# A long convolution beside a gated MLP: tokens by half-sequences, outer transforms in small array tiles, parameters in two plain loads, a new instruction order

## The chip, the core and the metric

One core of one Trainium2 chip. The metric is the device time of one execution in microseconds; the program runs on core 0 alone. What the host does with the arrays before the launch is not in it.

## What is computed

```python
xn = layernorm(A_u)                           # 2048 tokens x 512 channels, bf16
dt = exp(log_dt)[:, None]
K  = einsum("dn,dnl,dn->dl", C, exp(dt * A * l), dt * B).real   # A, B, C complex, 512 x 128
y  = irfft(rfft(pad(xn)) * rfft(pad(K)))[:2048] + xn * Dskip    # causal convolution, per channel
h  = sigmoid(xn @ w_gate) * (xn @ w_up)       # 2048 x 1792
out = A_u + y + h @ w_down                    # 2048 x 512
```

## The kernel before

**The two halves of the work.** The gated MLP takes the normalised tokens in four groups of 512. A group has 14 gate blocks (`fg`, L1026) and 14 up blocks (`fu`, L1041), each of four 128x512 matmuls, and four down projections (`fd`, L1074) of 14 matmuls each. ACT takes the sigmoid of a gate block out of PSUM (L1035). DVE multiplies it by the up block (L1056), either straight from PSUM or, for the units named in `UEV`, from SBUF after ACT has copied it there (L1052).

**The convolution.** Its 2048-point transform is split into an outer transform over 64 blocks and an inner one over 32. The parameters A, B, C and `log_dt` are loaded first (six DMA transposes, L445, and a broadcast load). ACT and DVE make from them the powers of exp(dt A) (the ladder, L666 to L680) and, for four chunks of 128 channels, two tables G and H by complex products (`cmul`, L731 to L737, and squarings, L788 to L794). PE multiplies the tables (`f_k`, L820, 128x32 column tiles) and selects rows of the product (`f_sel`, L842); that is the kernel K at 2048 lags. The outer transform of the tokens (`fm`, L695, one call for each of 16 token indices i) writes `z_scr` in DRAM through ACT (L697). After that the channels are done in two halves of 256 (p = 0, 1), each in eight units: load from `z_scr`, inner transform (L895, 64x64 tiles), an exchange of partitions by four 64 KB DMAs, transform of K (`fk`, L913), products on DVE (L919, L923), inverse inner transform (L936, 64x64 tiles), store to `v_scr`. The inverse outer transform (`s2_mm`, L994; L996 adds a correction for the last tokens) reads `v_scr` back.

**The layout of the tokens.** Token 16 p + i lies on partition p, index i. The outer transform mixes the 64 blocks of one parity, so `S1` and `S2` are 128x128 matrices in which one parity's rows or columns are zero, and each call makes two dense matmuls, one for each parity j:

```python
for j in range(2):
    T.matmul(bank(sl, j), s1[:, j, :], xn[:, i, :], start=True, stop=True)
```

**The end.** For tokens of groups 0 to 2 the MLP's result waits in SBUF, and `final` adds the two output transforms of a pair of indices to it (six pairs, L1009). For group 3 the output transform is added in PSUM behind the down projection (indices 12 to 15), and DVE adds the residual and stores (L1091). Index 15 is the last: its transform is made in two column halves behind its down projection, in the same PSUM bank, so that each half can be summed and stored alone.

**What sets the order.** Every piece of work is an `_Op`; `ORDER` is a list of their numbers written out by hand, and each engine runs its pieces in that order. PSUM buffers (two pairs of banks, three banks for gate and up, one for down) and SBUF buffers are handed out in the same order. DMAs are issued by SP, a few by ACT and POOL. `keep_warm` makes matmuls on zeros, 43 of them in four calls, without a consumer.

Of the kernel before, what the change touches and what calls it, by code (L numbers as in the profile page):

```python
# [13 lines left out]
ACT = mybir.ActivationFunctionType  # L14
# [5 lines left out]
L = 2048  # L20
# [155 lines left out]
def _consts():  # L176
# [16 lines left out]
    z1 = np.zeros((64, 2, 2, 128))  # L193
    z2 = np.zeros((128, 2, NA, 2))
    for j in range(2):
        z1[:, j, j, :] = s1
        z2[:, j, :, j] = _build_S2()
# [3 lines left out]
    sr = np.zeros((128, 4, 128))  # L201
    for q in range(8):
        sr[q, q // 2, 63 + 64 * (q % 2)] = 1.0
    return dict(SR=f(sr), ident=f(np.eye(128)), S1=f(z1.reshape(128, 2, 128)), S2=f(z2.reshape(128, 2, 128)), M2=f(quads(M2)), SW=f(sw),
                MAB=f(np.stack([quads(MA, True), quads(MB, True)], axis=2)), E=f(_build_E(M2).reshape(128, NU // 2, 2, NKT, 128).transpose(1, 0, 2, 3, 4)))

UEV = (18, 19, 27, 28, 29, 30, 31, 32, 33, 34, 35, 36, 37, 38, 39, 40, 41, 44, 45, 52)
ON_ACT = (0, 2)
ORDER = [
    1, 0, 4, 37, 38, 28, 47, 39, 27, 40, 41, 2, 3, 48, 49, 5, 50, 12, 29, 51, 17, 52, 53, 42, 23, 24, 26, 10, 44, 30, 31,  # L210
    43, 32, 7, 6, 45, 46, 33, 34, 107, 35, 19, 25, 134, 36, 54, 644, 55, 645, 632, 633, 58, 15, 14, 106, 634, 646, 685, 686,
    131, 11, 59, 695, 121, 696, 675, 680, 105, 108, 109, 94, 93, 676, 8, 22, 9, 92, 681, 132, 655, 638, 639, 656, 95, 96,
    60, 56, 660, 640, 661, 665, 110, 97, 135, 18, 16, 13, 670, 666, 672, 682, 61, 671, 120, 673, 119, 62, 683, 98, 684, 118,
    100, 650, 662, 663, 651, 674, 136, 102, 101, 99, 133, 63, 140, 664, 700, 647, 57, 652, 701, 64, 648, 122, 141, 653, 649,
    123, 654, 20, 690, 691, 180, 146, 692, 693, 657, 66, 103, 104, 142, 694, 667, 658, 65, 67, 668, 659, 669, 227, 68, 147,
    69, 635, 687, 688, 636, 677, 689, 678, 124, 637, 70, 679, 641, 143, 697, 72, 127, 642, 71, 702, 73, 643, 137, 703, 698,
    138, 74, 699, 704, 75, 76, 736, 705, 111, 731, 112, 77, 181, 228, 182, 229, 78, 706, 79, 733, 732, 230, 183, 707, 231,
    81, 139, 148, 80, 114, 734, 82, 708, 738, 735, 155, 83, 737, 128, 739, 232, 184, 84, 185, 740, 186, 85, 713, 87, 187,
    156, 781, 115, 714, 86, 88, 149, 751, 715, 90, 144, 113, 157, 188, 145, 190, 198, 782, 752, 709, 199, 193, 150, 783,
    161, 721, 723, 724, 152, 191, 200, 784, 722, 202, 785, 201, 153, 203, 725, 116, 233, 761, 206, 741, 176, 766, 207, 192,  # L220
    194, 762, 742, 125, 195, 767, 154, 151, 208, 117, 726, 756, 763, 177, 727, 757, 158, 162, 178, 209, 204, 771, 758, 210,
    764, 765, 759, 773, 167, 772, 205, 21, 163, 126, 189, 774, 760, 753, 728, 211, 729, 89, 775, 754, 214, 168, 196, 159,
    212, 129, 169, 730, 213, 160, 755, 215, 743, 746, 170, 164, 216, 744, 747, 91, 217, 218, 745, 171, 197, 219, 165, 234,
    788, 748, 749, 786, 787, 371, 166, 716, 220, 221, 222, 750, 235, 776, 130, 172, 778, 173, 237, 240, 789, 245, 246, 790,
    768, 249, 223, 247, 777, 248, 174, 250, 253, 175, 847, 224, 241, 238, 239, 242, 244, 769, 225, 779, 770, 780, 791, 254,
# [83 lines left out]

@with_exitstack  # L310
def kernel(
    ctx: ExitStack,
    tc: tile.TileContext,
    A_u: bass.AP,
    A_A_re: bass.AP,
    A_A_im: bass.AP,
    A_B_re: bass.AP,
    A_B_im: bass.AP,
    A_C_re: bass.AP,
    A_C_im: bass.AP,  # L320
    A_log_dt: bass.AP,
# [823 lines left out]
```

## Time and profile before

| | |
|---|---|
| median of 3 runs | 241.11 us (240.98 to 241.26) |
| profiled execution: span | 238.5 us, first to last instruction |
| around the span (median less span) | 2.6 us |
| PE busy | 227.5 us, 95% (of it L530, keep-warm: 11.6) |
| DVE busy | 187.5 us, 79% |
| ACT busy | 181.6 us, 76% |
| DMA | 43.60 MB, mean 183 GB/s |
| outer transforms, L695 | 32 dense matmuls of 128x512 |
| inverse outer transforms, L994 and L996 | 39 matmuls, 33 of 512 columns, 6 of 256 |

How to read it: matmuls are pipelined, so a matmul's listed duration (0.38 us for 512 columns) is longer than the time after which the next one starts (0.215 us). Costs on PE below are therefore start to start. The same holds on DVE and ACT to a smaller extent: one instruction starts about 0.1 us before the one ahead of it has ended.

### The profile page before, as it was taken

To read this page: it belongs to the slowest core of one execution; us is meant where nothing else is said; L and a number is where in the kernel's file an instruction comes from. 1 tells how busy PE (TensorE), PEld (TensorE's weight loads), DVE (VectorE), ACT (ScalarE), POOL (GpSimd) and SP (SyncE) were. 2 spreads that over 40 slices of the span, in tenths; PEclk is the share of its full clock that TensorE was granted. 3 is DMA by queue.
4 is the path that set the end of the run, shared out by engine and by line. 5 is a ranking of instruction groups with operands and counts; after the bars stand their busy time and mean duration, and the time that the engine had idled before them with its cause. 6 is when DMAs were issued, how large, how long until landed. Compare 5 with 4: busy or idle time off the path is not lost.

```text
span 238.5 us, 5382 instructions
## 1 busy us (share of the span) xinstructions
PE 227.5 (95%) x2074; PEld 113.8 (48%) x2074; DVE 187.5 (79%) x397; ACT 181.6 (76%) x294; POOL 18.4 (8%) x42
## 2 busy tenths in 40 slices
PE   7989999999999999999999999999999989799993
PEld 2455444444444454366545744436655455344441
DVE  3999899999999999999999999991334516672562
ACT  5999999999999997778998999976467878520000
POOL 1205210002000020100010500000000030000000
PEclk9999999999999999999999999999999999999999
DMA  5999795204366597474677386675677789579253
GB/s 155 223 355 328 229 353 133 91 0 88 132 168 219 162 179 206 85 214 88 204 162 215 91 237 183 185 214 128 187 198 197 222 168 275 157 198 290 98 193 104
DMA packets 50859, 43.60 MB, mean 183 GB/s; under 512 B 12561, under 2 KB 44050, under 8 KB 50834
## 3 DMA queue, kind: packets, MB, share of 16 engines
q1 hardware_dynamic: 48738, 40.58, 60.0%
q0 software_dynamic: 864, 1.57, 4.4%
q10 hardware_dynamic: 1232, 1.11, 1.4%
q8 instruction: 16, 0.26, 0.4%
q14 instruction: 9, 0.07, 0.1%
HBM read 24.64 MB, written 12.06 MB: 154 GB/s over the span
## 4 chain that ended last, share of the span: by engine, by line
PE 42%; ACT 24%; DMA 14%; DVE 7%; SPq 6%; issue 5%; ACTq 0%; DVEq 0%
PE bank L1074 15%; DMA big<-big 9%; PE bank L1026 7%; ACT hT_sb L1035 5%; SPq L417 4%; PE pair L913 4%; PE bank L1041 4%; ACT big L666 3%; PE pair L820 3%; ACT big L697 3%; DMA wg_sb<-in_B_w_gate_dram 3%; ACT big L672 3%; DVE big L919 2%; DMA big<-v_scr 2%; ACT big L558 2%
## 5 line engine op out<-in xcount | busy, mean ns | idle before, releaser
L1026 PE MATMUL bank<-xnT,wg_sb 128*128 128x512 bf16 (+1 forms) x236 | 55.4, 369 | 1.6 <-DMA wg_sb<-in_B_w_gate_dram 0.9
L1041 PE MATMUL bank<-xnT,wu_sb 128*128 128x512 bf16 x224 | 54.5, 380 | 0.1
L1074 PE MATMUL bank<-wd_sb,hT_sb 128*128 128x512 bf16 x224 | 51.0, 380 | 0.4 <-ACT glu_sb L1104 0.3
L1035 ACT ACTIVATE hT_sb<-bank 128x512 bf16<-128x512 f32 x56 | 33.2, 614 | 3.9 <-PE bank L1026 3.8
L1026 PEld LDWEIGHTS <-wg_sb 128*128 128x128 bf16 x236 | 21.5, 97 | 26.6 <-issue 5.1
L1074 PEld LDWEIGHTS <-hT_sb 128*128 128x128 bf16 x224 | 21.4, 98 | 26.3 <-issue 1.6
L1041 PEld LDWEIGHTS <-wu_sb 128*128 128x128 bf16 x224 | 21.2, 98 | 25.3 <-issue 2.0
L919 DVE TENSOR_TENSOR big<-big 128x2048 bf16<-128x2048 bf16 x16 | 19.4, 1219 | 16.1 <-DMA big<-big 6.8
L1056 DVE TENSOR_TENSOR hT_sb<-hT_sb,bank 128x512 bf16<-128x512 bf16 x36 | 24.0, 683 | 9.5 <-PE bank L1041 6.2
L731 DVE TENSOR_TENSOR big<-big 128x1024 bf16<-128x1024 bf16 (+4 forms) x40 | 25.9, 648 | 0.6 <-ACT big L772 0.3
L732 DVE TENSOR_TENSOR big<-big 128x1024 bf16<-128x1024 bf16 (+4 forms) x40 | 25.8, 646 | 0.0
L913 PE MATMUL pair<-big 128*128 128x256 bf16 x160 | 19.8, 273 | 0.4 <-DVE big L855 0.3
L900 ACT ACTIVATE big<-pair 128x1024 bf16<-128x1024 f32 x16 | 16.3, 1028 | 4.8 <-PE pair L895 4.7
L915 ACT ACTIVATE big<-pair 128x1024 bf16<-128x1024 f32 x16 | 16.5, 1035 | 3.9 <-PE pair L913 3.2
L940 ACT ACTIVATE big<-pair 128x1024 bf16<-128x1024 f32 x16 | 16.3, 1032 | 3.5 <-PE pair L936 1.7
L913 PEld LDWEIGHTS <-big 128*128 128x128 bf16 x160 | 15.5, 98 | 5.5 <-issue 1.1
L736 DVE TENSOR_TENSOR big<-big 128x512 bf16<-128x512 bf16 (+4 forms) x40 | 16.9, 424 | 0.2
L697 ACT ACTIVATE big<-pair 128x1024 bf16<-128x1024 f32 x16 | 16.9, 1058 | 0.0
L737 DVE TENSOR_TENSOR big<-big 128x512 bf16<-128x512 bf16 (+4 forms) x40 | 16.9, 422 | 0.0
L788 ACT ACTIVATE sq_sb<-big 128x256 bf16<-128x256 bf16 (+2 forms) x20 | 13.0, 657 | 2.4 <-DVE big L737 1.8
L936 PE MATMUL pair<-big 64*64 64x512 bf16 (+1 forms) x256 | 13.0, 327 | 1.4 <-DVE big L919 1.4
L772 ACT ACTIVATE big<-big 128x256 bf16<-128x256 bf16 x32 | 13.2, 459 | 1.0 <-PE pair L820 1.0
(106 smaller groups left out, 275.9 us busy)
## 6 DMA issues: line engine op xcount, KB each, us to landing
big<-c_E SPq DMA_DIRECT2D x16, 320.0 KB, 4.4
z_scr<-big SPq DMA_DIRECT2D x16, 256.0 KB, 2.6
big<-z_scr SPq DMA_DIRECT2D x16, 256.0 KB, 3.8
big<-big SPq DMA_DIRECT2D x64, 64.0 KB, 3.1
v_scr<-big SPq DMA_DIRECT2D x16, 256.0 KB, 3.5
big<-v_scr SPq DMA_DIRECT2D x12, 256.0 KB, 5.0
big<-in_A_u_dram SPq DMA_DIRECT2D x4, 512.0 KB, 5.2
wu_sb<-in_B_w_up_dram SPq DMA_DIRECT2D x2, 896.0 KB, 8.6
```

Source lines behind the costliest of these rows:

```text
L697: ev = pl.add("ACT", 0.90, lambda sl=sl, zs=zs: S.activation(out=zs().rearrange("p j d -> p (j d)"), in_=two(sl), func=ACT.Identity), [fx_ ...
L731: V.tensor_tensor(out=wide(outp), in0=wide(lo), in1=mre, op=ALU.mult)
L732: V.tensor_tensor(out=wide(tb()), in0=wide(lo), in1=mim, op=ALU.mult)
L736: V.tensor_tensor(out=outp[:, :, :, 0, :], in0=outp[:, :, :, 0, :], in1=tb()[:, :, :, 1, :], op=opr)
L737: V.tensor_tensor(out=outp[:, :, :, 1, :], in0=outp[:, :, :, 1, :], in1=tb()[:, :, :, 0, :], op=opi)
L913: T.matmul(two(sk)[:, o:o + DW], es()[:, g, kt, :], kT[p][:, kt, :], start=kt in (0, NKT - 1), stop=kt >= NKT - 2)
L919: V.tensor_tensor(out=pp().rearrange("p q h m -> p (q h) m"), in0=xx().rearrange("p q h m -> p (q h) m"), in1=kb()[:, 0:2 * DW].unsqueeze( ...
L1026: T.matmul(bank(sl)[:, c0:c1], w[:, kt, k * 128:(k + 1) * 128], xnT[:, grp, kt, c0:c1], start=(kt == 0), stop=(kt == KT - 1))
L1035: S.activation(out=hT_sb[:, hs.idx, k % 2, :], in_=bank(sl), func=ACT.Sigmoid)
L1041: T.matmul(bank(sl), wu_sb[:, kt, k * 128:(k + 1) * 128], xnT[:, grp, kt, :], start=(kt == 0), stop=(kt == KT - 1))
L1056: V.tensor_tensor(out=h(), in0=h(), in1=us_sb[:, us.idx, :] if on else bank(sl), op=ALU.mult)
L1074: T.matmul(bank(po), hT_sb[:, hts[k // 2].idx, k % 2, jj * 128:(jj + 1) * 128], wd_sb[:, k, :], start=(k == 0), stop=k == FT - 1, **kw)
```

## The change

- The host lays the tokens out so that partition 64 j + p' holds tokens 32 p' + 16 j + i: all blocks of one parity on one half of the partitions. The output is put back in order by the host.
- The outer transform of an index becomes four matmuls in 64x64 array tiles. The inverse outer transform becomes two matmuls in 128x64 column tiles, one for each parity.
- The host transposes the parameters and joins them to one array with the broadcast `log_dt`; the kernel loads it in two pieces, `log_dt` and A (384 KB) and B and C (512 KB).
- The last tile's down projection is split in two column halves with a PSUM bank each, and its output transform comes ahead of it.
- `UEV` names 28 units in place of 20.
- `ORDER` is another list. SP's queue now begins: `log_dt` and A; tokens 0 to 3 in two loads; tokens 4 to 11; the identity; tokens 12 to 15; the first part of w_gate; S1; B and C; the rest of w_gate; w_up; w_down. One call of 5 keep-warm matmuls stands behind some twenty blocks of the MLP. The output transforms stand in two stretches: pairs and late tiles 0, 12, 1, 13, 5 behind the second of group 3's down projections, and 3, 14, half of 15, 2, half of 15, 4 behind the third.

```diff
-    z1 = np.zeros((64, 2, 2, 128))
-    z2 = np.zeros((128, 2, NA, 2))
-    for j in range(2):
-        z1[:, j, j, :] = s1
-        z2[:, j, :, j] = _build_S2()
...
-UEV = (18, 19, 27, 28, 29, 30, 31, 32, 33, 34, 35, 36, 37, 38, 39, 40, 41, 44, 45, 52)
+UEV = (14, 15, 18, 19, 25, 27, 28, 29, 30, 31, 32, 33, 34, 35, 36, 37, 38, 39, 40, 41, 42, 43, 44, 45, 48, 50, 52, 55)
...
-        l_par[nm] = pl.add("SP", 1.27, lambda src=src, dst=rawn[nm]: Y.dma_start_transpose(dst, src), (), lp[0] + (0.055 if qi > 1 else 0.0),
-                           dma=(128 * KB, _rate(256), 0.5))
-        if qi == 1:
-            ld = at(OFF["G"] + 6 * KB, [D])
-            l_ld = load("SP", ld, A_log_dt.partition_broadcast(128), 128 * KB, pkt=1024)
-            l_id = load("SP", ident[:], cten["ident"].ap(), 32 * KB)
+    par = at(OFF["G"], [7, D])
+    ld, rawn = par[:, 0, :], {nm: par[:, 1 + qi, :] for qi, nm in enumerate(["Are", "Aim", "Bre", "Bim", "Cre", "Cim"])}
+    l_pa = load("SP", par[:, 0:3, :], A_par[:, 0:3, :], 384 * KB, pkt=3072)
+    l_id = load("SP", ident[:], cten["ident"].ap(), 32 * KB)
+    l_pbc = load("SP", par[:, 3:7, :], A_par[:, 3:7, :], 512 * KB, pkt=4096)
...
         def fm(i=i, sl=sl):
-            for j in range(2):
-                T.matmul(bank(sl, j), s1[:, j, :], xn[:, i, :], start=True, stop=True)
+            for o in (0, 64):
+                for j in range(2):
+                    T.matmul(bank(sl, j)[o:o + 64, :], s1[64 * j:64 * j + 64, o:o + 64], xn[64 * j:64 * j + 64, i, :], start=True,
+                             stop=True, tile_position=(64 * j, o))
...
-    def s2_mm(t, r, o, start, ps=(0, 1)):
+    def s2_mm(t, r, o, start, w):
         kw = dict(stop=True, skip_group_check=True)
         i = 2 * t + r
-        w = slice(DW * ps[0], DW * ps[-1] + DW)
+        ps = slice(w[0] // DW, w[1] // DW)
         for j in range(2):
-            T.matmul(o[:, w], s2[:, j, :], vall[:, t, ps[0]:ps[-1] + 1, j, r, :], start=start and j == 0, **kw)
+            T.matmul(o[64 * j:64 * j + 64, :], s2, vall[:, t, ps, j, r, :], start=start, tile_position=(0, 64 * j), **kw)
         if i >= 12:
-            T.matmul(o[:, w], sr[:, i - 12, :], rr[:, w], start=False, **kw)
+            T.matmul(o[64:128, :], sr[:, i - 12, :], rr[:, w[0]:w[1]], start=False, tile_position=(0, 64), **kw)
...
+            last = late and jj == 3
+            pos = [_Slot("gu" if late and jj % 2 else "po")] + [_Slot("gu")] * last
+            cols = [(0, 256), (256, 512)] if last else [(0, 512)]
...
+            for c, po in zip(cols, pos):
+                pre_ = []
+                if last:
+                    pre_ = [pl.add("PE", 0.23, lambda i=i, po=po, c=c: f2(i, po, c, True), ver, 30, acq=[po], mode="H")]
+                md = pl.add("PE", 3.03 if not last else 1.53, lambda fd=fd, po=po, c=c: fd(po=po, c=c),
+                            prods + [l_wd] + ([md] if jj else []) + ([mv_] if late else []) + pre_, DP, acq=[] if last else [po],
+                            rel=hts if jj == 3 and c[1] == 512 else [])
...
+def _rows(a):
+    return a.reshape(64, 2, NT, D).transpose(1, 0, 2, 3).reshape(128, NT, D)
```

## The prediction

> **What bounds the kernel now.** I read the table of stages first (busy time of each engine between the landmarks of the order list), then PE's timeline, then the DMA issues of the head.
>
> ```profile
> core 0: us, PE busy (x) PEld busy (x) DVE busy (x) ACT busy (x) POOL busy (x), PEclk, DMA share, GB/s
> 17.00:82.40 65.40, 63.82 (x292) 28.34 (x292) 63.31 (x138) 64.49 (x112) 7.17 (x12) 1.00 0.59 173
> 82.40:160.80 78.40, 77.77 (x1046) 41.46 (x1047) 77.87 (x174) 68.99 (x118) 6.43 (x15) 1.00 0.68 176
> 166.70:206.40 39.70, 37.44 (x310) 20.22 (x310) 16.87 (x21) 27.09 (x35) 2.24 (x3) 1.00 0.77 205
> 206.40:235.20 28.80, 28.18 (x151) 12.57 (x150) 15.20 (x26) 3.00 (x5) 0.00 (x0) 1.00 0.61 187
> ```
>
> 82.4 is the start of the first kernel product (L820), 166.7 of the first L913 of the second channel half, 206.4 of the last L936. PE is full in every stage. Up to 82.4 DVE and ACT are full with it, up to 160.8 DVE still is; after that PE is alone. So time is saved only by PE work removed, and before 160.8 only as far as DVE (the ladder, the tables) is not late. The granted clock is 1.00 throughout. The span is 238.5 us and the median of the runs 241.11: 2.6 us lie around the span. I keep them, and count changes of the span.
>
> **Array tiles.** The 16 outer transforms (L695) are two dense 128x512 matmuls each: 57.21 to 57.64, 0.43 us. In their place come four 64x64 tiles of 512 columns, and that shape is in the trace already: L895.
>
> ```profile
> 118.77 1.25 PE L913 MATMUL pair<-big 128*128 128x256 bf16 x10
> 119.95 0.41 PE L895 MATMUL pair<-big,m 64*64 64x512 bf16 x4
> 120.29 1.04 PE L1041 MATMUL bank<-xnT,wu_sb 128*128 128x512 bf16 x4
> ```
>
> The ten L913 take 10 x 0.109 = 1.09 us of issue, so the queue is free at 119.86. The tiles begin at 119.95 and the next dense block at 120.29: 0.43 us in all, of which 0.22 is 512 columns streaming, 0.09 the way in and 0.12 the way out. A lone tile block between dense blocks therefore costs what the two dense matmuls cost. Beside another tile block it is cheaper:
>
> ```profile
> 143.89 0.41 PE L895 MATMUL pair<-big,m 64*64 64x512 bf16 x4
> 144.13 0.82 PE L936 MATMUL pair<-big 64*64 64x512 bf16 x16
> 144.88 1.04 PE L1041 MATMUL bank<-xnT,wu_sb 128*128 128x512 bf16 x4
> ```
>
> 0.24 us to its neighbour. In the new order 12 transforms stand alone and 2 pairs stand together, 14 blocks: 16 x 0.22 + 14 x 0.21 = 6.4 us against 16 x 0.43 = 6.9. Gain **0.5 us** (between 0, if the drain is a little longer here, and 3.4, if it were hidden).
>
> [...]
>
> The new order also puts the old tile blocks (L895, L936, L820, L842) together more often: 23 stretches away from dense mode, against 30. 7 x 0.21 = **1.5 us** less (at least 0.7, since neighbours of unlike tiles may drain too).
>
> **Output transforms.** Now 6 pairs of four dense matmuls (L994, 0.86 us), three late tiles of three (0.65) and the last tile in two halves (0.33 each): 5.2 + 1.9 + 0.7 = 7.8 us. They become 128x64 column tiles, two side by side: 0.43 per pair, 0.43 per late tile (the L996 correction uses one tile alone), 0.22 per half: 2.6 + 1.3 + 0.4 = 4.3, and as the order holds them in two stretches, 2 x 0.21 for drains: 4.7 us. No row shows 128x64. The nearest is L842 (128x32, four side by side): 64 matmuls of 96 columns take 0.80 us, where one after another at 0.04 they would take 2.6. So column tiles do run side by side. Gain **3.0 us**; if two such tiles did not overlap, a loss of 0.4.
>
> [...] L842's loads take 96 ns against 97 for dense ones, so I add nothing.
>
> **Last tile.** Its down projection becomes 28 matmuls of 256 columns: 28 x 0.109 = 3.07 against 3.02. Its transform moves ahead of it, into two banks. Before, it is behind, in one bank:
>
> ```profile
> 230.64 3.18 PE L1074 MATMUL bank<-wd_sb,hT_sb 128*128 128x512 bf16 x14
> 233.66 0.38 PE L994 MATMUL bank<-big 128*128 128x256 bf16 x2
> 233.88 0.27 PE L996 MATMUL bank<-big 128*128 128x256 bf16 x1
> 234.67 0.38 PE L994 MATMUL bank<-big 128*128 128x256 bf16 x2 [0.52 <-DVE big L1091]
> ```
>
> The 0.52 us wait for DVE's read of the first half goes: **0.5 us**. What is late next is DVE's own last sum (0.42 us), as now.
>
> **Head.** The parameters go from six transposes and a broadcast to two plain loads, and SP is the queue they leave:
>
> ```profile
> 0.74 0.86 SPq L417 DMA_DIRECT2D big<-in_A_u_dram  x2
> 2.12 1.23 SPq L445 DMA_TRANSPOSE big<-in_A_A_re_dram  x1
> 9.89 0.43 SPq L417 DMA_DIRECT2D wg_sb<-in_B_w_gate_dram  x1
> 11.46 3.32 SPq L445 DMA_TRANSPOSE big<-in_A_C_re_dram  x1
> ```
>
> At 0.48 us an issue the last weight load is issued by about 8 us instead of 19. PE transposes at 11.58, begins L1026 at 14.2 and waits for wg_sb until 17.04; with the weights there it could run through from about 13.5, when the layer norms let it, and be 1.4 us ahead at that mark. But DVE is as full as PE up to 82.4, and the work ahead of the first L820 in the list is the same on it but for one L1056 product that reads SBUF (0.42) instead of PSUM (0.68). DVE begins at 3.79, when the first 256 KB of tokens land; the two token loads land 0.64 us apart. Now 384 KB of parameters go first, then ACT's exponential (0.61) runs, and DVE's first product waits for both: 3.8 + 0.3 + 0.6 = 4.7. I take **+0.9 us** for the first L820 (between -1.4, if PE's start decides, and +1.6). PE's head start then turns into idle time, and the new order has 5 of the warm-up matmuls in the middle of it.
>
> Toward 160.8 DVE's list is 2.0 us shorter than before (one pair of L919/L923, 1.74 us, comes later, and products read SBUF). From the third L820 (130.72) to the first L913 of the second half (166.66) PE has 34.6 us of listed work in 35.9 us; I count half of that 1.3 us as won: **-0.7**.
>
> ACT gets 8 more evictions of the up projection (8 x 0.48 start to start, 3.8 us), DVE 8 x 0.27 less. Those before 160.8 fall on ACT's 9 us of slack there, the others where it is busy 27.1 of 39.7 us. Nothing; with that cover gone, up to 3.8.
>
> **Second half and its loads.** Between the first L913 of the second half and the last L936 the list now queues 8576 KB of DMA against 6720, since the stored halves v_scr are read back sooner. The stage moved 205 GB/s at a share of 0.77, so some 266 at full; the longer list needs nearly that. I add **+0.8** (0 to 2.5). In exchange only 2 MB of loads stay behind the last L936. Its eviction, store and first load took from 206.44 to 217.4, 768 KB of other loads ahead of it; without them about 3 us less, 8 us. PE has 0.75 + 1.72 + 0.28 + 3.02 + 0.32 + 3.02 = 9.1 us of work until the first output transform, and the third, fourth and fifth loads land at about 1 us each: **+0.8** (0 to 2).
>
> **Sum.** -0.5 - 1.5 - 3.0 - 0.5 + 0.9 - 0.7 + 0.8 + 0.8 = -3.7 us: span 234.8, time **237.4 us**.
>
> **Rivals.** (1) PE's earlier start counts: the new order keeps DVE and ACT from being late at 82.4, and the -1.4 stands in place of +0.9: 235.1. For it: weights land far earlier, and ACT has the same load. Against it: DVE's start is later and its list equal. Chance 0.22. (2) The column tiles run one after the other: -3.0 becomes +0.4, 240.8. Against it: L842. Chance 0.07. (3) Slower: the second half becomes DMA-bound. The list's 6720 KB (6.9 MB) in 39.7 us are 173 GB/s where the profile counts 205, a factor of 1.18; so 8576 KB are about 10.4 MB, at 266 GB/s 39 us, just within PE's 40.5 (37.9 of listed work and the 2.6 idle of now). It decides once the rate falls below 257, and the whole gain is eaten at 235; at 205, the rate of now, the stage is 51 us, some 10 more: 247. For it: many of these are 64 KB swaps, and DVE waits for them there already. Against it: the share was 0.77, not 1. Chance 0.10. (4) Tile switching and the new waits cost what the rest brings, 241 within 0.2%: 0.05. Forecast: 0.56.
>
> **How the numbers follow.** The forecast's own bounds, and rival 1, reach to 234.3 below; above, rival 2 with a little of the DMA wait is 240.9. Outside lie rival 3 and the tails. 0.2% is 0.5 us, about what can be told from no change. Faster: forecast, rival 1 and most of rival 2, 0.84; same 0.05; slower 0.11.
>
> **What would show it.** Right: transforms as 64x64 blocks of 0.43 us alone; L994's successor in two stretches of about 2.2 us; the first 128x82 products at about 83.3; no wait in the last tile; PE's last matmul near 231. Wrong: first products before 82 (rival 1), output transforms of 0.86 (rival 2), waits of DVE for swaps and a DMA share near 1 between 167 and 207 (rival 3).

## The result and the profile after

The changed kernel takes 240.17 us, median of 20 executions, against 240.93 of the kernel before on the same chips. The ratio is **0.9946, interval 0.9923 to 0.997**: 1.3 us faster, where -3.7 was forecast. (The ratios leave out executions more than 1.5% above the fastest of their kernel, the medians hold all; that is why the two differ.) A second measurement on another chip gave 0.9957 (0.9926 to 0.9987). The profiled execution takes 238.51 us with a span of 236.7, so 1.8 us lie around the span and not the 2.6 that I took from the runs of before; the spans differ by 1.8 us.

From the page of the changed kernel, the busy time of each engine:

```profile
PE 220.5 (93%) x2093; PEld 112.2 (47%) x2120; DVE 184.5 (78%) x397; ACT 184.2 (78%) x302; POOL 26.0 (11%) x42
```

PE's busy time is 220.5 us against 227.5 before. But 27 of its matmuls have no record here (x2093 beside x2120 weight loads), and the time of a missing one can count as idle. Two of the runs below have every record and the full clock: no_acc, with the same order on PE, and old_order.

```profile
PE 224.6 (95%) x2120; PEld 112.1 (47%) x2120; DVE 184.7 (78%) x397; ACT 184.6 (78%) x302; POOL 17.2 (7%) x40
```

```profile
PE 224.1 (95%) x2120; PEld 111.7 (47%) x2120; DVE 187.4 (79%) x397; ACT 181.1 (77%) x294; POOL 18.4 (8%) x42
```

So the work that went is some 3 us and not 7, and part of it became waiting. The table by stage, cut at the same landmarks as in the prediction (first kernel product, fourth chunk's kernel product, first E product of the second half (L898, the transform of K), last inverse product, PE's end):

```profile
core 0: us, PE busy (x) PEld busy (x) DVE busy (x) ACT busy (x) POOL busy (x), PEclk, DMA share, GB/s
17.00:81.60 64.60, 63.07 (x310) 26.01 (x315) 63.39 (x139) 64.34 (x111) 6.51 (x12) 1.00 0.49 149
81.60:160.90 79.30, 76.64 (x1027) 42.26 (x1039) 76.34 (x174) 69.83 (x121) 14.66 (x15) 1.00 0.64 169
169.30:209.00 39.70, 37.04 (x300) 20.08 (x306) 16.49 (x22) 29.13 (x39) 1.78 (x2) 1.00 0.79 227
209.00:233.60 24.60, 21.34 (x160) 10.90 (x161) 13.70 (x24) 2.52 (x3) 0.00 (x0) 1.00 0.71 204
```

The order has moved work between the stages (from the fourth chunk's product to the first E product PE is busy 7.7 us where it was 5.6), so the length of a stage is not yet a gain or a loss. At 209.0 two blocks of inverse products stand together; the last, which is the landmark of before, begins at 209.64. The tail is 24.6 us instead of 28.8, but 3.3 of them are without PE, against 0.6. The longest of PE's waits:

```profile
PE pair L880 <- DMA big<-z_scr: 2.1, 1, 2.1
```

PE's waits of over 0.35 us behind the warm-up sum to 8.6 us; before they sum to 4.6. New are two ahead of the output transforms (L979, 1.65 and 1.47 us) and three of 0.66, 0.56 and 0.63 us at the selection products (L827). A second profile of the same kernel (after_again) has the two of the tail again, 1.69 and 1.46 us, but only 0.43 us for `z_scr`, which took 0.87 before. The tiles themselves are as costed. PE's timeline (start, us, what, and in brackets the idle time before it), a lone forward transform and the tail:

```profile
15.30 0.71 PE L1011 MATMUL bank<-xnT,wg_sb 128*128 128x256 bf16 x5
15.94 0.41 PE L679 MATMUL pair<-big 64*64 64x512 bf16 x4
16.28 0.82 PE L1011 MATMUL bank<-xnT,wg_sb 128*128 128x256 bf16 x5
...
220.79 0.62 PE L979 MATMUL pair<-big 128*64 128x512 bf16 x4 [1.65 <-DMA big<-v_scr]
222.88 0.41 PE L979 MATMUL bank<-big 128*64 128x512 bf16 x2 [1.47 <-DMA big<-v_scr]
...
224.73 3.20 PE L1064 MATMUL bank<-wd_sb,hT_sb 128*128 128x512 bf16 x13
...
230.35 3.23 PE L1064 MATMUL bank<-wd_sb,hT_sb 128*128 128x256 bf16 x28
```

The output transforms run from 220.79 with 0.45, from 222.88 to 224.73 and from 227.85 to 230.35: 4.8 us, and 4.7 was forecast. The last tile's 28 products of 256 columns end without a wait. But the first stretch waits twice for loads, and the down projection of 3.2 us that could cover them stands behind it, at 224.73. Before, the first transform stood at 217.46 and a down projection directly behind it, at 218.31:

```profile
217.46 1.02 PE L994 MATMUL pair<-big 128*128 128x512 bf16 x4
218.31 3.19 PE L1074 MATMUL bank<-wd_sb,hT_sb 128*128 128x512 bf16 x14
```

### The profile page after: what moved, and what is told of

Same layout as the page of the kernel before. It is cut to its first block, busy times and chain, and to the rows that moved or that the text cites. A ratio compares the mean times of both kernels' runs of the same rounds, so it can differ in the third digit from the quotient of the medians.

```text
span 236.7 us, 5439 instructions
## 1 busy us (share of the span) xinstructions
PE 220.5 (93%) x2093; PEld 112.2 (47%) x2120; DVE 184.5 (78%) x397; ACT 184.2 (78%) x302; POOL 26.0 (11%) x42
## 5 line engine op out<-in xcount | busy, mean ns | idle before, releaser
L1026 PE MATMUL bank<-xnT,wu_sb 128*128 128x512 bf16 x209 | 52.9, 379 | 2.1 <-DVE hT_sb L1041 0.8
L1064 PE MATMUL bank<-wd_sb,hT_sb 128*128 128x512 bf16 (+1 forms) x231 | 50.6, 367 | 0.5 <-DVE hT_sb L1041 0.2
L1011 PEld LDWEIGHTS <-wg_sb 128*128 128x128 bf16 x236 | 22.1, 98 | 26.2 <-issue 4.4
L1064 PEld LDWEIGHTS <-hT_sb 128*128 128x128 bf16 x238 | 22.4, 98 | 24.7 <-issue 2.1
L1026 PEld LDWEIGHTS <-wu_sb 128*128 128x128 bf16 x224 | 20.6, 98 | 26.6 <-issue 5.4
L1020 ACT ACTIVATE hT_sb<-bank 128x512 bf16<-128x512 f32 x56 | 32.6, 611 | 0.0
L716 DVE TENSOR_TENSOR big<-big 128x1024 bf16<-128x1024 bf16 (+4 forms) x40 | 25.9, 647 | 0.7 <-ACT big L757 0.5
L898 PE MATMUL pair<-big 128*128 128x256 bf16 x160 | 19.6, 273 | 0.0
L1041 DVE TENSOR_TENSOR hT_sb<-hT_sb,bank 128x512 bf16<-128x512 bf16 x28 | 18.4, 682 | 0.3 <-PE bank L1026 0.3
L898 PEld LDWEIGHTS <-big 128*128 128x128 bf16 x160 | 15.6, 98 | 4.6 <-issue 0.2
L1037 ACT ACTIVATE us_sb<-bank 128x512 bf16<-128x512 f32 x28 | 16.7, 610 | 1.0 <-DVE hT_sb L1041 0.7
L757 ACT ACTIVATE big<-big 128x256 bf16<-128x256 bf16 x32 | 13.8, 450 | 0.6 <-PE pair L805 0.6
## 6 DMA issues: line engine op xcount, KB each, us to landing
wu_sb<-in_B_w_up_dram SPq DMA_DIRECT2D x2, 896.0 KB, 10.4
```

The source lines that it names most:

```text
L716: V.tensor_tensor(out=wide(outp), in0=wide(lo), in1=mre, op=ALU.mult)
L898: T.matmul(two(sk)[:, o:o + DW], es()[:, g, kt, :], kT[p][:, kt, :], start=kt in (0, NKT - 1), stop=kt >= NKT - 2)
L1011: T.matmul(bank(sl)[:, c0:c1], w[:, kt, k * 128:(k + 1) * 128], xnT[:, grp, kt, c0:c1], start=(kt == 0), stop=(kt == KT - 1))
L1020: S.activation(out=hT_sb[:, hs.idx, k % 2, :], in_=bank(sl), func=ACT.Sigmoid)
L1026: T.matmul(bank(sl), wu_sb[:, kt, k * 128:(k + 1) * 128], xnT[:, grp, kt, :], start=(kt == 0), stop=(kt == KT - 1))
L1037: S.activation(out=us_sb[:, us.idx, :], in_=bank(sl), func=ACT.Identity)
```

## The experiments

All are the changed kernel with one edit, a few with two. Groups of them were measured beside the kernel before on one chip, different groups on different chips; between groups a difference of half a per cent is not much (the same kernel, old_order, has 0.9887 and 0.9852). In their lines a line number is often one less than in the changed kernel. Where only `ORDER` changes, the diff gives the moved numbers.

| run | median us | before | ratio, interval |
|---|---|---|---|
| after_again | 239.86 | 240.63 | 0.9957 (0.9926 to 0.9987) |
| order_only | 246.13 | 240.55 | 1.0185 (1.0136 to 1.0234) |
| old_order | 238.56 | 240.91 | 0.9887 (0.9844 to 0.993) |
| old_order_2 | 237.08 | 240.45 | 0.9852 (0.9814 to 0.989) |
| dense_s2 | 243.64 | 240.25 | 1.0123 (1.0087 to 1.0159) |
| dense_fx | 243.67 | 240.63 | 0.9982 (0.9946 to 1.0019) |
| transposes | 242.16 | 240.25 | 1.0102 (1.006 to 1.0144) |
| acc_early | 243.75 | 240.25 | 1.0127 (1.0082 to 1.0171) |
| no_acc | 241.38 | 240.55 | 1.003 (1.0002 to 1.0057) |
| noloadwait | 238.92 | 240.63 | 0.9931 (0.9897 to 0.9965) |
| tail2 | 239.99 | 240.55 | 0.9973 (0.9946 to 1.0001) |
| tail3 | 239.9 | 240.91 | 0.9938 (0.9903 to 0.9973) |
| p0_late | 239.37 | 240.91 | 0.9903 (0.9864 to 0.9942) |
| p0_tail3 | 242.2 | 240.91 | 1.0051 (1.0023 to 1.0079) |
| p0_cover | 240.55 | 240.45 | 0.9982 (0.9948 to 1.0017) |
| filler | 239.3 | 240.63 | 0.9912 (0.988 to 0.9944) |
| sel_later | 243.25 | 240.25 | 1.0102 (1.0058 to 1.0146) |
| sel3 | 240.42 | 240.55 | 1.0014 (0.9981 to 1.0047) |

### The order or the edits

**order_only.** Both outer transforms dense, the new order and the rest kept (the two diffs of dense_fx and dense_s2 below, together).

> The changed kernel with both outer transforms dense again, forward and inverse: what is left of the change is the new order, the layout by half-sequences, the plain parameter loads and the halves of the last tile. Theory I (the tiles bring what was forecast, 3 to 3.5 us of TensorE's work, and the new order by itself costs): 1 to 1.5 % slower than the kernel before, about 4 us slower than the changed kernel. Theory J (the order costs nothing and the tiles bring little): within 0.5 % of the kernel before.

1.85% slower than before, 4.5 us. Theory I: the new order without the tiles is a loss. In part that is the clock, of which more below (a mean of 0.986 to 0.993 in four of its six executions); but the two at full clock, 243.78 and 245.4 us, are also 3 to 5 us above the kernel before.

**old_order** and **old_order_2** (the same kernel twice).

```diff
-UEV = (14, 15, 18, 19, 25, 27, 28, ...)
+UEV = (18, 19, 27, 28, 29, 30, 31, ...)      # the kernel before's
 ORDER = [
-    2, 42, 43, 19, ...
+    ... the list of the kernel before, each operation by its number here
+    ... tile 15: both halves of its transform, then its two half products
```

> The changed kernel's code (half-sequences, both outer transforms in array tiles, plain parameter loads, the last tile in halves) with the order of the kernel before, operation for operation, and its choice of evictions; of the last tile the two halves of the transform stand ahead of its two half products. With the run that had the new order alone (1.85 % slower than before), it splits the change in two. Theory I (the tiles bring about 3.5 us wherever they are put, the new order costs): 2.5 to 4 us faster than the kernel before, 1 to 2.5 us faster than the changed kernel. Rival M (the tiles only pay in an order made for them: in the old one TensorE waits where the dense products were cover): within 1 us of the kernel before.

> The kernel of old_order once more, for a narrower interval (it had 7 executions): the changed code in the old order. Theory I: 2 to 3 us faster than the kernel before, no execution at 0.993 or below. Rival: the first measurement was a good chip, and it lies within 1 us of the changed kernel's 0.9946 to 0.9957.

0.9887 and 0.9852: **2.7 and 3.6 us faster than the kernel before**, and faster than the changed kernel in both. These are the lowest ratios of this study, though p0_late below comes close (0.9903, on old_order's chip). That they come near the forecast's -3.7 is in part chance: its terms for these edits (-0.5, -3.0, -0.5) make -4.0, and the rest of it belongs to the new order and the head. The last two stages of old_order_2, and PE at its first output transform:

```profile
167.20:206.50 39.30, 37.31 (x305) 20.15 (x310) 16.77 (x21) 26.96 (x35) 2.24 (x3) 1.00 0.76 205
206.50:232.40 25.90, 25.16 (x162) 12.09 (x164) 15.14 (x25) 3.13 (x5) 0.00 (x0) 1.00 0.64 205
```

```profile
217.47 0.62 PE L978 MATMUL pair<-big 128*64 128x512 bf16 x4
218.02 3.19 PE L1063 MATMUL bank<-wd_sb,hT_sb 128*128 128x512 bf16 x14
```

Its waits sum to 4.4 us, little less than before the change, and no transform waits for a load: there is no wait ahead of the first, and a down projection stands behind it. (In old_order's profile the first transform waits 0.72 us.) Up to the last inverse product it keeps the times of the kernel before (206.54 against 206.44); the gain lies in the tail, 25.9 us instead of 28.8. That is the -3.0 of the column tiles, and the last tile's 0.5 against a new wait of 0.51 us for VectorE. The changed kernel's PE waits 4.2 us more than this one's. What its tile blocks save by standing together is less: without the keep-warm products PE is busy 212.1 us in no_acc and 212.9 in old_order, the two profiles above.

**dense_s2.** The inverse outer transforms dense again.

```diff
-T.matmul(o[64 * j:64 * j + 64, :], s2, vall[...], start=start, tile_position=(0, 64 * j), **kw)
+T.matmul(o, s2[:, j, :], vall[...], start=start and j == 0, **kw)
```

> The changed kernel with the inverse outer transforms as dense 128-wide products again, two products of half zeros where the changed kernel has two column tiles; everything else, the order too, as changed. If column tiles run side by side, the listed TensorE work is about 3 us more. Theory A (the transforms' work is on the path, and the waits for v_scr between them are not longer than the work saved): span about 2 to 3 us longer than 236.7. Rival B (the transforms wait for v_scr anyway, so that a part of the saved work only became waiting): 0.5 to 2 us longer, and the waits ahead of the transforms shorter than 1.65 and 1.47 us. Rival C (column tiles one after the other): no difference.

1.0123 against 0.9946 and 0.9957 of the changed kernel: about 4 us, the 3.0 of the forecast and one more, again partly by the clock (0.991 to 0.993 in five of six). Rival C is out.

**dense_fx.** The forward outer transforms dense again.

```diff
-            for o in (0, 64):
-                for j in range(2):
-                    T.matmul(bank(sl, j)[o:o + 64, :], s1[64 * j:64 * j + 64, o:o + 64], xn[...], ..., tile_position=(64 * j, o))
+            for j in range(2):
+                T.matmul(bank(sl, j), s1[:, j, :], xn[:, i, :], start=True, stop=True)
```

> The changed kernel with the forward outer transforms as two dense products of 128 by 512 each, instead of four tiles of 64 by 64. My forecast has the edit at -0.5 us (a lone block 0.43 us either way, only the pairs save): 0 to 0.7 us longer than the changed kernel on the same chip. Rival (four tiles at once take the time of one dense product, half the work): 16 blocks by 0.215 = 3.4 us longer.

0.9982 against 0.9957 on the same chip: 0.6 us, as forecast (each interval reaches 0.7 to 0.9 us to either side, so it can't be told from nothing), and far from the 3.4 of the rival. The medians of all executions lie 3.8 us apart: nine of dense_fx's twelve have a mean clock of 0.993 or less, and six of the changed kernel's twelve. At full clock they are 239.94 us (three executions) and 239.33.

**transposes.** The parameters by six transposing loads and a broadcast, where the two plain loads stand.

> The changed kernel with the parameters again loaded by six transposing loads and a broadcast, in the place in the queue of the two plain loads. Theory A (the plain loads are why VectorE ends the tables of chunk 0 in time, 81.6 us for the first kernel product): the first table instruction comes 0.5 to 1.5 us later and the first kernel product with it, span 0.5 to 1.5 us longer than 236.7. Rival B (ScalarE and TensorE are full until 81 us and VectorE has room): first product within 0.3 us, span within 0.4 us. Rival C (transposes slow the loads of the weights beside them): the first gate product at 13.6 us is late by 0.5 us or more.

The first kernel product comes at 86.09 us instead of 81.6 to 83.8 with the plain loads. TensorE waits 1.72 us at 11.2 and 1.70 at 14.0, and its granted clock (the column behind POOL) is 0.50 from the second wait until 21.4:

```profile
17.60:21.00 3.40, 3.40 (x18) 1.89 (x17) 3.30 (x9) 2.52 (x5) 0.00 (x0) 0.50 0.95 301
```

So the plain loads are needed in this order; Theory A, and more than its 1.5 us. How much of it is VectorE's later start and how much the clock (0.993 or less in all six executions) was not separated.

### The tail

**acc_early.** GpSimd's last two accumulating loads issued at 185.7 and 186.3 us instead of 206.7 and 207.3.

```diff
 ORDER: ... 953, 949,
+ 883, 884, 876,                 # eviction dE:11, acc:11, acc:9
 512, 513, ... 530,
- 883,
 537, ... 901,
- 884,
 566, ... 964,
- 876,
 620, ...
```

> The changed kernel with three entries of the order moved: ScalarE's eviction dE:11 and GpSimd's accumulating loads acc:11 and acc:9 stand at about 182 us, as soon as their sums are complete, and not at 205 to 207 us. Theory A (the late accumulating loads hold up the last two stores of v_scr): the last two stores land about 2 us after their issue instead of 4.4 and 4.1, the two waits of TensorE ahead of the output transforms (1.65 and 1.47 us) shrink to about 1 us together, the span falls by about 2 us from 236.7. Rival B (the tail is bound by the rate at which the last loads of v_scr come, 204 GB/s in that stage): the stores land sooner, the waits only move to later transforms, span within 0.5 us of 236.7. Rival C (the bytes were only moved): the second pass waits longer for its z_scr load at 200 us than the 2.15 us of now, and that takes back more than half.

The last two stores take 2.3 and 3.5 us from issue to landing (4.7 and 4.5 in the changed kernel) and the tail's waits fall from 3.1 to 1.8 us, as Theory A has it. But the 512 KB now collide with the second pass's loads (Rival C), TensorE waits 3.47 us there, and the clock halves:

```profile
191.40:194.80 3.40, 0.00 (x0) 0.00 (x0) 0.70 (x1) 0.60 (x1) 0.00 (x0) 1.00 1.11 317
194.80:198.20 3.40, 3.33 (x24) 1.38 (x25) 2.77 (x5) 2.05 (x2) 0.00 (x0) 0.50 0.95 252
```

**no_acc.** The same two loads left out.

```diff
 def facc(i=i, fx=fx):
+    if i in (9, 11):
+        return
```

> The changed kernel without the last two accumulating loads on GpSimd (output tiles 8 to 11 then lack the input that these add). Theory A (they hold up the last two stores of v_scr, which landed 4.4 and 4.1 us after their issue): the stores land about 2 us after their issue, the time from the last pair of inverse products to the first output transform falls from 11.8 to about 10.2 us (all cover, no wait), TensorE's waits in the tail from 3.1 to about 1.5 us, the time by 1.5 us. Rival H (the rate of the loads behind the stores decides): stores sooner, the waits of the later transforms larger by the same, time within 0.5 us of the changed kernel.

The DMA view, last two stores, in the kernel before, the changed kernel and this one (KB each, median us from issue to landing):

```profile
v_scr<-big SPq DMA_DIRECT2D x2, 256.0 KB, 2.3
```

```profile
v_scr<-big SPq DMA_DIRECT2D x2, 256.0 KB, 4.6
```

```profile
v_scr<-big SPq DMA_DIRECT2D x2, 256.0 KB, 3.6
```

By these the accumulating loads would be 1.0 us of the 2.3 by which the stores are later. But the changed kernel's second profile (after_again) has the stores as early with the loads, issued there 6 us ahead of the stores and not 4 to 5:

```profile
v_scr<-big SPq DMA_DIRECT2D x2, 256.0 KB, 3.4
```

So what the loads cost is not shown. In the profile the tail's waits fall to 2.0 us and PE's way from the last inverse product to its end by 1.1 us, but its second pass is 1.0 us longer (40.7 against 39.7) and the time shows no gain. What delays the stores stays open; one difference was not tried: they are issued 0.9 us apart, and before 1.9.

**noloadwait.** The second half's loads read the first half's store.

```diff
-v_v = v_scr[p][:].rearrange(...)
+v_v = v_scr[0][:].rearrange(...)
```

> The changed kernel with the loads ahead of the output transforms reading, for the second half of the channels, the store of the first half, which was complete long before (that half of the output is another's numbers). The same bytes are loaded, but the loads no longer wait for the last two stores. Theory A (the wait for the last stores is what the tail lost): the two waits of TensorE of 1.65 and 1.47 us go, the time from the last pair of inverse products to TensorE's end falls from 24.6 to about 21.5 us, the time by about 3 us against the changed kernel on the same chip. Rival B (the loads are bound by the rate at which they come): the loads are issued earlier but collide with the second pass's own, the second pass grows, the time falls by less than 1.5 us.

The wait did not go. SyncE's queue, with the loads behind a store that waits for ScalarE's eviction (which waits 3.35 us itself, until an earlier store has landed), and what TensorE then shows:

```profile
213.37 4.73 SPq L407 DMA_DIRECT2D v_scr<-big  x2
218.15 2.19 SPq L407 DMA_DIRECT2D big<-v_scr  x3
```

```profile
PE pair L979 <- DMA big<-v_scr: 2.8, 1, 2.8
```

Taking the data dependence away leaves the queue's order. I had not named that wait, and the run can't price the dependence.

**tail2** and **tail3.** More cover ahead of the transforms, transforms by landing (s2 t is the output transform of the pair of indices t).

```diff
-pos = [_Slot("gu" if late and jj % 2 else "po")] + ...
+pos = [_Slot("gu" if late and jj else "po")] + ...
 # tail2, TensorE: ... down 13, down 14, s2 1, s2 0, tiles 12, 13, s2 5, s2 3, 14, 15, 15, half product, s2 2, s2 4, half product
 # tail3, TensorE: ... down 13, s2 1, s2 0, s2 5, down 14, tiles 12, 13, s2 3, 14, 15, 15, s2 2, half product, s2 4, half product
```

> The changed kernel with another order of its tail: the third of the last four down projections (tile 14, 3.2 us) stands before the output transforms and not between them, in a bank of its own; the transforms then stand in the order in which their loads land (t = 1, 0, 6, 5, 3, 7, 2, 4); the load for t = 4 is issued with the others. Theory F (the tail lost its gain because the transforms became shorter than the loads they wait for, and 3.2 us of cover lie behind them and not ahead): TensorE's waits of 1.65 and 1.47 us go, at most 1 us stays for VectorE, which adds each pair in 1.13 us; time 2 to 2.5 us below the changed kernel, and no halved clock in the tail. Rival G (VectorE becomes the bound: eight sums of 1.13 and five of 0.3 to 0.6 us behind the first transform): 0 to 1 us below.

> The changed kernel with the tail ordered by landing: transforms for t = 1, 0 and 5 as their loads land, then the third of the last four down projections (3.2 us, a bank of its own), then the rest; the load for t = 4 issued with the others. Theory F (cover stands behind the waits): TensorE waits about 1.4 us in the tail instead of 3.1, VectorE sums the first three pairs beside the down projection, time 1.5 to 2.5 us below the changed kernel. Rival G (VectorE's sums and the three output buffers are the next bound, as in the run with all cover ahead, which gained 2.1 us on TensorE and 0.3 at the end): 0 to 0.7 us below.

In tail2 PE's way from the last inverse product to its end falls from 24.6 to 22.5 us, but the way to the end of the span only from 27.7 to 27.5. VectorE is next, and its output buffers:

```profile
233.56 1.22 DVE L993 TENSOR_TENSOR big<-pair,glu_sb 128x1024 bf16<-128x1024 f32 x1 [0.42 <-DMA out_dram<-big]
```

tail3 waits 1.90 and 0.62 us in its profile. Neither is clearly faster than the changed kernel (0.9973 and 0.9938). Rival G for both. The tail has three limits close together: the landing of the loads, PE, and VectorE's eleven sums.

**p0_late, p0_tail3, p0_cover.** Three of the first half's loads (768 KB) behind the last store; then with tail3's order; then with a down projection between the first transform and the others.

```diff
 ORDER (SyncE): ... 607, 575, 576,
+ 613, 621, 615,
 614, ...                          # and taken out of the second pass
```

> The changed kernel with the last three of the first half's v_scr loads (256 KB each, issued at 191.5, 193.4 and 203.4 us, among the second pass's own loads) moved on SyncE's queue behind the last store, where the DMA engines stand still from 215 to 218.5 us. Theory N (the second pass is held by the 768 KB that were put into it): its z_scr and E loads land sooner, the wait of TensorE at 198 to 203 us (0.4 to 2.2 us in the runs so far) goes to 0.5 us or less, the stretch from the first E product to the last inverse products falls from 39.7 (38.3 to 41.1 in unchanged second passes) to about 38, the tail stays, time 0.5 to 1.5 us below the changed kernel. Rival O (they then hold up the last loads instead): the tail longer by as much.

> Both edits of the two kernels before this one together: the three loads moved into the tail, and the tail ordered by landing. If N and F hold and do not meet: 2 to 4 us below the changed kernel, about 236 to 238 us. If the moved loads delay the last loads, no better than the better of the two alone.

> The changed kernel with the three first-half loads behind the last store (as in p0_late), and the third of the last four down projections between the first output transform, whose load lands first, and the others, whose loads land 2.5 to 6 us later: 3.2 us of work where p0_late waited 3.41 us and then ran 6.7 us at half clock. Theory (the second pass gains 1.5 us by the bytes taken out of it, and the tail's wait, with the halved clock that follows it, goes when work stands in its place): no execution at 0.99 or below from the tail, time 2 to 3.5 us below the changed kernel, about 236.5 to 237.5. Rival G (VectorE's sums and the three output buffers end last): the end no earlier than p0_late's undisturbed executions, 237.9.

The stretch from the first E product to the last inverse product is 38.25, 38.0 and 38.0 us in the three, 39.7 in the changed kernel's first profile, 38.25 in its second: Theory N is not shown. In p0_late the tail waits 3.4 us in one piece:

```profile
222.87 0.64 PE L978 MATMUL bank<-big 128*64 128x512 bf16 x2 [3.40 <-DMA big<-v_scr]
```

Its ratio of 0.9903 is still a little better than the changed kernel's (the intervals overlap), and the 5 of its 12 executions that kept the full clock have a median of 237.85 us. In p0_tail3 the transform for t = 1 stands first, and with the moved loads t = 0 lands first: a wait of 2.95 us, and every one of 12 executions below full clock. p0_cover has 2.21 us ahead of the first transform and no gain. The landing order that I had planned for was that of another run.

### The clock

**after_again** and **filler.** The changed kernel once more, and with products in its waits.

```diff
 def fm(...):
+    if p == 1 and u == 5:
+        for _ in range(8): T.matmul(two(sl)[:, 0:512], glu_sb[:, 0, 0:128], glu_sb[:, 0, :], start=True, stop=True)
 def fy():
+    if t == 0:
+        for _ in range(10): T.matmul(bank(sl, 0), glu_sb[:, 0, 0:128], glu_sb[:, 0, :], start=True, stop=True)
```

> The changed kernel as it is, beside the others on one chip. In two of the four runs so far (three variants of it, and the one with transposing loads) TensorE waited 2 to 3.5 us in one piece or in two close ones, and the profile then shows a granted clock of 0.50 for about 3.5 us, mean 0.991. Theory D (the changed kernel's longer waits of TensorE in the second pass and the tail, 2.15, 1.65 and 1.47 us, are long enough to halve the clock in some executions): among the executions of one kernel, those with a mean clock of 0.993 are about 1.7 us longer than those with 1.000 (half of 3.4 us), and the kernel before, whose longest wait is 1.43 us, has none at 0.993. Rival E (the clock follows the chip and not the kernel): before shows the same share of 0.993. Time about 239.5 to 241.

> The changed kernel with 8 products (1.7 us) whose sums are overwritten, issued on TensorE ahead of the transform that waits 2.15 us at 198.5, and 10 (2.2 us) ahead of the first output transform, which waits 1.65 us and has a wait of 1.47 us behind it. They work only while TensorE would have waited. Theory D (waits of about 2 us and more halve the clock for 3.4 us in some executions): no execution at 0.993 or below, median 0.5 to 1 us below the changed kernel on the same chip, highest time lower by 1.5 us or more. Rival E (the clock does not depend on them): as the changed kernel, or up to 1 us longer for products that did not fit a wait.

Stages of after_again's tail; the waits are 1.69 us at 219.2 and 1.46 us at 221.5:

```profile
219.20:223.00 3.80, 0.66 (x7) 0.21 (x6) 1.22 (x1) 0.52 (x1) 0.00 (x0) 0.89 0.99 309
223.00:227.00 4.00, 4.00 (x15) 1.44 (x17) 1.73 (x3) 0.00 (x0) 0.00 (x0) 0.50 0.65 215
```

The granted clock is 0.50 right behind the two waits. A mean clock of 0.993 or less, which such a stretch of 3.4 us leaves (0.5 x 3.4 of 238), is found in 9 of the changed kernel's 20 executions, in 6 of 12 here, in 1 of 12 with the filler, in 0 of 13 of the old order, and in 3 of 122 of the kernel before. Theory D, though it had expected none with the filler and none of the kernel before. In after_again the executions at full clock have a median of 239.33 us, those at 0.993 of 240.28, those at 0.985 to 0.986 of 243.8. The filler's ratio is 0.9912 against 0.9957 on the same chip: 1.1 us.

### The middle

**sel_later** and **sel3.** Selection products later; the inverse product mab:3 (a block of inverse inner transforms) behind the last selection.

```diff
 # sel_later
-ORDER: ... 862, 219, 740, ...          +... 786, 219, 220, ...
-ORDER: ... 336, 324, 313, 834, 858, 314, 339, ...   +... 859, 313, 314, 473, ...
 # sel3
-ORDER: ... 359, 424, 360, 873, ...     +... 359, 360, 424, 873, ...
```

> The changed kernel with the selection products of state chunk 0 moved behind the next down projection, and those of chunk 2 behind the next up projection, on TensorE; nothing else. It takes away the two waits of 0.66 us at 89.6 us and 0.56 us at 141.1 us for a pair of PSUM that an eviction on ScalarE still holds. Theory A (TensorE is the bound there): both waits go, span 1.0 to 1.2 us shorter than 236.7. Rival B (VectorE's ladder sets the pace between 80 and 161 us, TensorE's waits only move): the product starts of chunks 1 and 3 (103.1 and 160.9 us) stay, span within 0.4 us. Rival C: the later selection makes the next ladder late, and the span grows by up to 1 us.

> The changed kernel with the inverse product mab:3 moved behind the selection products of chunk 3. In every trace so far TensorE stops 0.4 to 0.7 us some 3.5 us into the block of about 400 short products that begins with chunk 3's kernel products (161 us), with no releaser recorded. Theory K (TensorE's own instruction stream runs dry in long runs of short instructions): the stop stays at about the same count of instructions, now inside mab:3 or the selection. Theory L (the selection waits for a buffer): the stop stays at the selection's start, or goes. Time within 0.7 us of the changed kernel.

sel_later: the way from the first chunk's kernel product to the second's grows from 21.5 to 23.3 us; Rival C, the ladder needs the selection where it is; the loss is more than the 1 us that Rival C allowed, and four of the six executions have a clock of 0.985 to 0.993. So the waits of 0.66 and 0.56 us are not cheap to remove. For the third, of 0.63 us, PE's timeline of the changed kernel and of sel3 (the chunk's kernel products begin at 160.91 and 162.51):

```profile
165.92 0.37 PE L827 MATMUL pair<-big,sw 128*32 128x96 bf16 x17 [0.63 <-issue]
```

```profile
167.56 0.20 PE L826 MATMUL pair<-big,sw 128*32 128x96 bf16 x1 [0.44 <-issue]
```

The stop without a releaser comes 191 matmuls after the chunk's first kernel product in both (128 + 16 + 47 and 128 + 63), whichever work stands there; in old_order one of 0.73 us comes 188 matmuls into another chunk. That fits Theory K (the instruction stream), and is not proof of it.

## Why the prediction was right and wrong

**Right: the costs of the tiles.** -0.5 for the forward transforms: a lone block takes 0.43 us in the trace (five products from 15.30 take 5 x 0.109 us of issue, to 15.85, and the next dense block begins at 16.28), and dense_fx costs 0.6. (What the 0.21 us beside the columns' 0.22 are, which the prediction calls a drain, no run shows; the traces have their length.) -3.0 for the column tiles: 4.8 us of stretches against 4.7, and 4.0 us in dense_s2. -0.5 in the last tile: no wait is left. Rival 2 (columns in turn) is out. All edits in the old order: -2.7 and -3.6, for terms of -4.0 (the -0.5 of the forward transforms does not show there: up to the last inverse product nothing is gained).

**Not tried alone: the blocks put together (-1.5).** Between no_acc and old_order PE's busy time differs by 0.8 us: about the term's lower bound of 0.7.

**Wrong: the terms of the new order.** I gave it -0.7 in the middle, +0.8 in the second pass and +0.8 in the tail, +0.9 together, and credited it with the -1.5. By the runs the order costs about 2 us more than the old one with the same code (0.9946 and 0.9957 against 0.9887 and 0.9852, 1.4 to 2.5 us, on different chips); with dense transforms it is 4.5 us slower than the kernel before.

- *Tail, +0.8.* This is the step that failed: "without them about 3 us less, 8 us". From the start of the last block of inverse products the sum had 9.1 us of work until the first transform, and 8 until its load. Measured are 9.5 us of work (209.64 to 219.14), and the load lands just ahead of 220.79, 11.1 behind that start; the next load costs 1.47 more. That makes 3.1 us of waits and not 0.8. The way from that start to the first transform was 11.0 us before. Its parts: until the last store is issued 2.16 us, now 2.23; until it has landed 2.40, now 4.47; from there to the transform, which is the load, 6.46, now 4.45. So the 768 KB of other loads, taken out of the way, brought 2.0 of the 3 us that I had counted, and the store, which I had left as it was, took 2.1 more. In the second profile the parts are 3.57, 3.30 and 4.52 us and the whole is 11.4: the length repeats, its parts don't. The issue of the last store, before and after, and the stretch in which the changed kernel's stores end and its loads begin, where the DMA engines have little to do:

```profile
208.60 0.36 SPq L417 DMA_DIRECT2D v_scr<-big  x1
```

```profile
211.87 0.36 SPq L407 DMA_DIRECT2D v_scr<-big  x1
```

```profile
215.00:218.30 3.30, 3.30 (x19) 1.39 (x17) 0.00 (x0) 0.00 (x0) 0.00 (x0) 1.00 0.13 29
```

  And the transforms, halved, now need a pair of loads in 0.43 us where the loads land 0.5 to 1.4 us apart, so part of what they save is waited away behind the first (1.47 us, and 0.60 with dense transforms in dense_s2). In the old order a down projection stands there. No run shows what a tail without these waits would bring: tail2 took them away, and VectorE then ended last.
- *Middle, -0.7.* From the third kernel product to the first E product it is 36.0 us (133.29 to 169.26), before 35.9: nothing was won. I read 1.3 us of idle PE before as winnable and did not look for waits that the new order makes: selections that ask for a PSUM pair while ScalarE still evicts (0.66, 0.56) and a stop of 0.63 us.
- *Second pass, +0.8.* Up to the last block of inverse products, the landmark of before, it is 40.4 us in the first profile, 39.1 in the second and 39.8 before: the term is neither shown nor refuted. Rival 3 (DMA-bound) did not come, at a share of 0.79 and 227 GB/s: 9.0 MB, where 10.4 had been estimated.
- *Head, +0.9.* VectorE did begin at 4.79 us, as worked out, but the first kernel product came at 81.63, at 82.85 in the second profile (82.0 to 82.9 in most other runs), and not at 83.3; before it came at 82.44. So +0.9 did not show, nor rival 1's -1.4: the head is within 0.8 us of before, and at the fourth chunk's product nothing is left of that (160.91 against 160.79).
- *The clock.* The prediction had none of it: a wait of TensorE was priced at its length.

Put together, roughly: -0.5 - 0.8 - 3.0 - 0.5 for the work, nothing for head, middle and second pass, +3.1 for the tail: -1.7 us, and the span fell by 1.8. The tail alone is 2.3 us over its term; the blocks and the middle are 0.7 each over theirs, and head and second pass together 1.7 under.

## What to carry to other kernels

When work on the bounding engine is cut behind a chain of store, load and use, the work was also the chain's cover: price the chain alone. In the old order a down projection stands between the first use and the rest; in the new one, putting it there (p0_cover, with other loads moved too) or ahead of the uses (tail2) brought nothing clear, since VectorE's sums and the other loads come close behind. A new order is an edit of its own; the old order with the new code is the run that shows its price, and here that is the version to keep. Where TensorE waits, look at the granted clock behind the wait: here, behind waits of 1.69 and 1.46 us and with a clock of 0.50, the way from the second wait's end to the start of the last tile's down projection took 10.4 us (after_again, 222.99 to 233.35), and 7.5 us at 1.00 in the first profile (222.88 to 230.35): 2.9 us more for 3.15 us of waits.

## What the runs showed of the hardware

- TensorE's granted clock was 0.50 for 3.4 us from the end of a wait of 3.47 us on (acc_early, 194.8 to 198.2), and for 6.8 us from within the second of two waits on: of 1.69 and 1.46 us with 0.6 us of work between them (after_again, 222.2 to 229.0), and of 1.72 and 1.70 us with 1.1 us between them (transposes, 14.6 to 21.4). In the changed kernel's first profile it stayed at 1.00 behind waits of 2.15, 1.65 and 1.47 us; 9 of that kernel's 20 executions have a mean of 0.993 or less. In which of them it falls is open.
- Two 256 KB stores to DRAM took 2.3 us to land in the kernel before and 4.6 in the changed one, where GpSimd had issued two accumulating loads of 256 KB 4 to 5 us ahead; 3.4 with these 6 us ahead, 3.6 without them. What sets it is open.
- In a run of matmuls that are mostly short (82 and 96 columns) TensorE stopped 0.63 us (the changed kernel, 165.92) and 0.44 us (sel3, 167.56) with no releaser behind 191 of them, the same count in two orders.
